# Gathering token rows by quarters and turning them on VectorE in front of six experts

## The chip, the cores and the metric

The kernel runs on one core of a Trainium2 chip. The metric is the device time of one execution in microseconds (us). The core has TensorE (PE, with its weight loads shown as PEld), VectorE (DVE), ScalarE (ACT), GpSimd (POOL) and SyncE (SP), which here issues most of the DMA transfers; GpSimd issues the transfers that go by a list of indices. A matmul reads its operands from SBUF and writes into one of eight banks of PSUM.

## The reference

An attention of the RWKV kind gives 4 x 768 = 3072 token rows of 8 x 48 = 384 channels. A router then picks one of eight experts for each token, and the expert is a two-layer network, applied with the router's weight:

```python
xn = x / (np.linalg.norm(x, axis=-1, keepdims=True) + 1e-06)
logits = xn @ en.T / tau                  # en: normalised expert embeddings, 8 x 384
expert_idx = np.argmax(logits, axis=1)
gate_w = softmax(logits)[np.arange(N), expert_idx]
for e in range(E):                        # 8 experts, F = 1024
    mask = expert_idx == e
    h = np.maximum(x[mask] @ w1[e], 0.0)  # w1[e]: 384 x 1024
    out[mask] = gate_w[mask, None] * (h @ w2[e])  # w2[e]: 1024 x 384
```

## The kernel before

The attention comes first, in 12 turns. Each finished chunk of token rows goes to a scratch array `xs` in DRAM (3072 x 384, f32) and through the router. When all tokens have an expert, VectorE has a list of token numbers for each expert, sorted by the experts' size: `take` holds, for expert e and tile t, the 128 token numbers of the tile, one per partition. `goes` holds where their results go.

The experts are worked off in this order with fixed capacities (CAPS, in tokens): 384, 384, 432, 416, 400, 384, 384, 384. Below, experts are numbered by it from 0 to 7. Experts 0 and 1 (`EARLY`) start before the last lists are there, and their first layer is done by plain products (L1065, L1070). Experts 2 to 7 take these steps:

- **Gather** (`gather`, L1037). GpSimd issues an indirect DMA per tile: up to 128 rows of 384 channels (1536 bytes) from `xs` into a tile G, token on partition. There are eight such tiles, four for even experts and four for odd ones.
- **Turn** (`turn_m`, L1134). A product contracts over partitions, so the channels have to come onto partitions: TensorE multiplies each 128 x 128 block of G by the identity, three column blocks m, into the PSUM banks Y. ScalarE copies each m to SBUF (`copy_x`, L1127) as `xTe[:, m, :]`.
- **First layer** (`group`, L1157). Two groups of 2 x 2 block products by Strassen's scheme, which needs sums of blocks of the weights (S, `sum_w1`) and of x (Tx, `sum_x`), both by VectorE in the helper at L1087. The results, after an add by VectorE and a relu by ScalarE, are hT (or RT, the same role for odd experts).
- **Second layer** (`layer2`). First the last tile's third (L1320) or, at over 384 tokens, its columns (L1327), then again Strassen's block products (L1290), with sums of h (RT on VectorE, `sum_h`) and of w2 (T, `sum_w2`). The adds at L1312 and a scaling at L1374 write y rows, which GpSimd scatters to the output (`send`, L1259).

The weights of an expert come by SyncE: w1 as three DMAs of 128 partitions x 1024 (512 KB each), w2 as four (L1023). Two sets of weight tiles alternate. Weights of expert e + 2 are issued when expert e's second layer has been written out.

The order of instructions on every engine is fixed by hand: `plan.at(t, f, ...)` files a step under a time, and `plan.emit()` writes the steps in order of these times. Each engine works its instructions off strictly in that order and waits for what an instruction needs. So a step's planned time says only where it stands in its engine's queue. In `experts` the turning of the next expert's x stands at the end of each expert's first layer (at + 0.0, 0.4, 2.7), around the third or the columns of the second layer. The matmuls that open a new accumulation take the next of six PSUM banks in a ring (`ring_bank`); the two banks Y are kept for the transposes.

Of the kernel before, what the change touches and what calls it, by code (L numbers as in the profile page):

```python
# [11 lines left out]
I32 = mybir.dt.int32  # L12
# [170 lines left out]
def build_consts(k):  # L183

    nc, pool = k.nc, k.const
    k.half = pool.tile([128, B], F32, name="half")
    nc.gpsimd.memset(k.half, 0.5)
    k.casts = []
    k.token = pool.tile([128, NCH, B], I32, name="token")
    nc.gpsimd.iota(k.token, pattern=[[C * B, NCH], [C, B]], base=0, channel_multiplier=1)  # L190

    k.ng = pool.tile([128, NCH, B, 2], F32, name="ng")
    k.rev = numbers(k, "rev", [128, E], [[-1, E]], E, 0)
    k.slot = numbers(k, "slot", [128, 128], [[1, 128]], 0, 0)
# [12 lines left out]
    k.rev_sorted = pool.tile([128, E], F32, name="rev_sorted")

    k.cum_oh = pool.tile([128, E, B + 1], F32, name="cum_oh")
    nc.gpsimd.memset(k.cum_oh[:, :, 0:1], 0.0)  # L210
    k.cum = k.cum_oh[:, :, 0]
    k.oh = k.cum_oh[:, :, 1:].rearrange("q x b -> q b x")
    k.on = pool.tile([128, E, B + 1], F32, name="on")
    nc.gpsimd.memset(k.on, 1.0)
    nc.gpsimd.memset(k.on[:, :, 0:1], 0.0)
    k.back = pool.tile([128, NCH, B], F32, name="back")
    k.rank = pool.tile([128, NCH, B], F32, name="rank")
    k.lists = pool.tile([128, E, 2, TM], F32, name="lists")
    nc.gpsimd.memset(k.lists[:, :, 0, :], float(SKIP))
    nc.gpsimd.memset(k.lists[:, :, 1, :], 0.0)  # L220
    k.lists_sorted = pool.tile([128, E, 2, TM], F32, name="lists_sorted")
    k.take = pool.tile([128, E, TM], I32, name="take")
    k.goes = pool.tile([128, E, TM], I32, name="goes")
    k.take_first = pool.tile([128, EARLY, AHEAD], I32, name="take_first")


def cast_consts(k):
# [525 lines left out]
        k.nc.vector.reduce_sum(k.take_first[:, :, i], t, axis=AX.X)  # L753


def goes(k):
    out_rows(k, k.goes, k.take, k.rt)

# [78 lines left out]
def attention(k):  # L837
# [115 lines left out]
    for t, fn, *args in (  # L953
        (14.1, logits, k, c),
        (15.2, take_logits, k, c),
        (16.1, turn_logits, k, c),
        (16.2, keep_logits, k, c),
        (16.6, choose, k, c, True),
        (18.0, ranks, k, c),
        (18.7, placed, k, c),  # L960
        (18.8, places, k, c),
        (18.6, choose_a, k, c),
        (19.0, scale, k, c),
        (19.9, rows_of, k, c),
        (20.25, exps, k, c),
        (20.9, gate, k, c),
        (21.0, values, k, c),
        (21.5, sort_lists, k),
        (l + 4.5, put, k, c),
        (l + 5.5, collect, k, c),  # L970
        (l + 5.6, goes, k),
        (l + 5.9, flags, k),
    ):
        plan.at(end + t, fn, *args)
# [24 lines left out]
    plan.at(P + 6.9, embeddings_a, k)  # L999
    plan.at(P + 8.7, cast_consts, k)  # L1000
    plan.at(2 * P + 6.0, embeddings_b, k)
    plan.at(2 * P + 6.6, embeddings_c, k)
    plan.at(2 * P + 7.6, decays, k)
    for i, G in enumerate(k.G):
# [8 lines left out]
def weights(k, j, which, pieces=None, paced=False):  # L1013

    w = k.weights[j][which]
    e = bass.ds(k.expert[j], 1)
    if which == 0:
        src, step = k.w1[e].rearrange("o (c p) f -> p (o c) f", p=128), 1
    else:
        src, step = k.w2[e].rearrange("o (f p) m -> p (o f) m", p=128), 2  # L1020
    all_pieces = range(0, src.shape[1], step)
    for m in all_pieces if pieces is None else all_pieces[pieces]:
        ins = k.nc.sync.dma_start(out=w[:, m : m + step], in_=src[:, m : m + step])  # L1023
        if paced:
            after(k, ins, k.last)
# [6 lines left out]
def gather(k, e, t):  # L1032
    n = rows_in(e, t)
    G = k.G[(e % 2) * TM + t]
    first = e < EARLY and t < AHEAD
    rows = (SETTLE[t] + 1) * B * C if first else N
    k.nc.gpsimd.indirect_dma_start(  # L1037
        out=G[0:n, :], out_offset=None, in_=k.xs[0:rows, :],
        in_offset=IndirectOffsetOnAxis(ap=(k.take_first if first else k.take)[0:n, e, t : t + 1], axis=0),
        bounds_check=rows - 1, oob_is_err=False,  # L1040
    )


# [73 lines left out]
def sum_x(k, e, i):  # L1117
# [3 lines left out]
        return  # L1121
    t = [k.T1[:, j, 0:h] for j in range(4)]
    right_sums(k, t, [[half_of(k, e, m, c) for c in range(2)] for m in range(2)], i)


def copy_x(k, e, m):
    k.nc.scalar.copy(x_of(k, e, m)[:, 0 : CAPS[e]], k.xbank[m][:, 0 : CAPS[e]])  # L1127


def turn_m(k, e, m):  # L1130
    ps = k.xbank[m] = k.Y[m % 2]
    for t in range(TILES[e]):
        G, r = k.G[(e % 2) * TM + t], rows_in(e, t)
        k.nc.tensor.transpose(  # L1134
            ps[:, t * 128 : t * 128 + r], G[0:r, m * 128 : (m + 1) * 128], k.ident[0:r, 0:r]
        )


def group(k, plan, e, g, at):
# [251 lines left out]

def experts(k):
    nc = k.nc
    k.turn = 5
    k.sent = 0
    k.outs = dram_disjoint_views(k.out, 4)
    k.xT = [k.gp1.tile([128, NK, max(CAPS)], F32, name=f"xTe{i}") for i in range(2)]
    wide = [k.gp1.tile([128, NF // 2, max(CAPS)], F32, name=f"hT{i}") for i in range(2)]
    rt = [x.rearrange("q u p s j i -> q (u p s j i)") for x in k.RT]
    k.h = [wide, [x.rearrange("q (f i) -> q f i", f=4) for x in rt[0:2]]]  # L1400
# [4 lines left out]
    k.T1 = k.gp1.tile([128, 5, max(CAPS) // 2], F32, name="Tx")  # L1405
    k.T2 = k.gp1.tile([128, 4, 4, 192], F32, name="T2")
    k.kept = [k.gp1.tile([128, max(CAPS)], F32, name=f"kept{i}") for i in range(3)]
    k.xbank = {}
    for e in range(EARLY):
        for t in range(AHEAD, TILES[e]):  # L1410
            turn_tile(k, e, t)
    for e in range(EARLY):
        for t in range(TILES[EARLY + e]):
            gather(k, EARLY + e, t)
    nc.gpsimd.drain()
    for e in range(EARLY):
        layer1_rest(k, e)
    plan = Plan()
    at = 0.0
    for e in range(E):  # L1420
        if e >= EARLY:
            for g in range(2):
                group(k, plan, e, g, at + g * GROUP * CAPS[e] / 384)
# [6 lines left out]
        nxt = {0: 2, 1: None}.get(e, e + 1)  # L1430
        if nxt is not None and nxt < E:
            for m in range(NK):
                plan.at(at + (0.0, 0.4, 2.7)[m], turn_m, k, nxt, m)
                plan.at(at + (0.45, 0.9, 3.0)[m], copy_x, k, nxt, m)
            for t in range(TILES[nxt + 1] if EARLY <= e and nxt + 1 < E else 0):
                plan.at(at + 3.1, gather, k, nxt + 1, t)
            for i in range(5):
                plan.at(at + (4.0, 5.8, 6.2, 7.6, 8.4)[i], sum_x, k, nxt, i)
            at += 0.9
# [273 lines left out]
def kernel(  # L1713
# [37 lines left out]
    sets = [weight_tiles(n, i) for i in range(2)]  # L1751
    n.weights = [sets[e % 2] for e in range(E)]
    n.expert = {}
    n.G = [n.const.tile([128, DM], F32, name=f"G{i}") for i in range(2 * TM)]

    with tc.manual_schedule(), ExitStack() as long_ctx:
        n.long = long_ctx.enter_context(tc.tile_pool(name="long", bufs=1))
# [39 lines left out]
```

## Time and profile before

| | us |
|---|---|
| median of 3 runs | 408.48 |
| lowest and highest | 408.22, 412.2 |
| the profiled execution | 407.85 |
| its span, first to last instruction | 406.0 |
| TensorE busy | 385.4 (95%) |
| VectorE busy | 227.0 (56%) |
| ScalarE busy | 146.0 (36%) |
| GpSimd busy | 130.6 (32%) |
| granted TensorE clock | 0.992 of full speed |

The profile's page shows one execution. Its groups of instructions name the source line, the engine, the operation, output <- inputs by the program's names, then count, busy time and what ended the idle time before them. "PE py L1134" in the chain of waits is work of TensorE into a tile named py by line 1134. A piece of the chain is given by its start, its length, what it is, and how many instructions it holds. In a timeline row, the number in brackets is the time for which the engine was idle before the instruction, and behind the arrow stands what it waited for. "issue" is time in which it waited for nothing that the profile shows. The line numbers in these rows are those of the kernel before; in the changed kernel the same code stands some 60 lines lower.

### The profile page before, as it was taken

How to read it: one execution, taken by the hardware profiler on the slowest of the kernel's cores; microseconds unless marked ns; L12 is line 12 of the kernel's file. 1: busy time of each engine (PE TensorE's matmuls, PEld its weight loads, DVE VectorE, ACT ScalarE, POOL GpSimd, SP SyncE). 2: the span in 40 equal slices, each digit the busy share in tenths (PEclk: the TensorE clock that was granted, in tenths of full speed). 3: DMA queues.
4: the chain of work that ended last, by engine and by line, in shares of the span. 5: the costliest groups of instructions: out<-in, count | busy, mean ns of one | idle time of the engine just before them, and what ended most of it. 6: DMA issues, size and time to landing. Idle time of an engine off the chain costs nothing.

```text
span 406.0 us, 12451 instructions
## 1 busy us (share of the span) xinstructions
PE 385.4 (95%) x5116; PEld 346.1 (85%) x5116; DVE 227.0 (56%) x578; ACT 146.0 (36%) x375; POOL 130.6 (32%) x167
## 2 busy tenths in 40 slices
PE   8879989899997999999999999999999999999993
PEld 4767879797887999978899999999998889979983
DVE  6866777788788380433752644546454464374331
ACT  3355554555462634321134214313413413413410
POOL 2765746474542231612151023104303412012001
PEclk9999999999998999999999999999999999999998
DMA  9998787777606357825743252424605553001001
GB/s 126 172 167 168 160 175 165 164 167 162 162 26 214 118 182 238 271 95 180 280 137 111 84 194 89 150 58 160 207 21 183 151 177 119 0 19 39 2 19 48
DMA packets 95460, 54.40 MB, mean 134 GB/s; under 512 B 78723, under 2 KB 90034, under 8 KB 95394
## 3 DMA queue, kind: packets, MB, share of 16 engines
q1 hardware_dynamic: 89634, 43.68, 42.1%
q0 software_dynamic: 3264, 9.44, 7.0%
q10 hardware_dynamic: 2496, 0.40, 0.8%
q8 instruction: 42, 0.69, 0.7%
q14 instruction: 24, 0.20, 0.1%
HBM read 44.20 MB, written 9.58 MB: 132 GB/s over the span
## 4 chain that ended last, share of the span: by engine, by line
PE 82%; DMA 4%; issue 3%; DVE 1%; POOL 0%; POOLq 0%; SPq 0%
PE ps L1157 15%; PE ps L1290 12%; PE pu L1157 8%; PE ps L1070 5%; PE pu L1290 5%; PE ps L371 4%; PE ps L1320 4%; PE ps L411 4%; PE ps L1327 3%; PE pu L536 3%; PE pu L1320 3%; PE py L502 2%; PE py L1070 2%; PE py L1134 2%; PE pu L447 2%
## 5 line engine op out<-in xcount | busy, mean ns | idle before, releaser
L1259 POOL DMA_INDIRECT out_dram<-y,goes x27 | 30.8, 1141 | 173.7 <-ACT y L1374 91.9
L1037 POOL DMA_INDIRECT G<-xs,take x23 | 24.4, 1061 | 29.4 <-PE py L1057 8.5
L1157 PE MATMUL ps<-xTe,w 128*128 128x192 f32 (+3 forms) x160 | 31.4, 333 | 0.0
L355 POOL TENSOR_TENSOR Rw<-R,rpow 128x384 f32<-128x384 f32 x22 | 23.1, 1051 | 16.6 <-PE ps L411 8.4
L1157 PEld LDWEIGHTS ps<-xTe,w 128*128 128x128 f32 x160 | 27.5, 190 | 0.0
L1312 DVE SCALAR_TENSOR_TENSOR y<-ps,lists_sorted,kept 128x192 f32<-128x192 f32 x18 | 7.1, 416 | 36.0 <-ACT kept L1304 22.2
L1070 PE MATMUL ps<-RT,w 128*128 128x128 f32 x204 | 26.2, 278 | 0.7 <-DVE RT L1060 0.4
L1290 PE MATMUL ps<-T,RT 128*128 128x192 f32 x144 | 26.0, 328 | 0.0
L1070 PEld LDWEIGHTS ps<-RT,w 128*128 128x128 f32 x204 | 24.2, 192 | 1.5 <-issue 0.6
L411 PE MATMUL ps<-RT,KT 48*64 48x128 f32 x768 | 25.0, 274 | 0.3 <-issue 0.2
L1290 PEld LDWEIGHTS ps<-T,RT 128*128 128x128 f32 x144 | 23.6, 190 | 0.6 <-ACT kept L1304 0.6
L411 PEld LDWEIGHTS ps<-RT,KT 48*64 48x64 f32 x768 | 21.0, 133 | 3.7 <-issue 2.7
L351 POOL TENSOR_TENSOR Kw<-K,kpow 128x384 f32<-128x384 f32 x22 | 23.5, 1068 | 0.0
L1157 PE MATMUL ps<-Tx,S 128*128 128x192 f32 (+3 forms) x96 | 20.3, 341 | 0.0
L387 ACT COPY RT<-ps 128x512 f32<-128x512 f32 x22 | 12.9, 586 | 19.9 <-PE ps L371 17.9
L1175 ACT COPY kept<-ps 128x384 f32<-128x384 f32 (+3 forms) x24 | 11.7, 490 | 22.7 <-PE ps L1157 19.7
L1087 DVE TENSOR_TENSOR RT<-ps,kept 128x384 f32<-128x384 f32 (+1 forms) x15 | 8.5, 566 | 19.9 <-PE ps L1157 19.9
L426 DVE TENSOR_TENSOR AT<-ps,smask 128x256 f32<-128x256 f32 x48 | 18.5, 413 | 1.1 <-PE ps L411 1.1
L398 DVE TENSOR_TENSOR RT<-ps,uw 128x512 f32<-128x512 f32 x22 | 15.2, 689 | 6.8 <-ACT RT L387 6.7
L371 PE MATMUL ps<-ident,Rw 128*128 128x128 f32 x96 | 15.4, 282 | 3.6 <-POOL Rw L355 1.6
L1127 ACT COPY xTe<-py 128x384 f32<-128x384 f32 (+3 forms) x18 | 8.8, 490 | 27.0 <-PE py L1134 26.9
L433 DVE COPY_PREDICATED AT<-dmask,ps 128x256 f32<-128x256 int32 x48 | 18.5, 439 | 0.0
(344 smaller groups left out, 889.9 us busy)
## 6 DMA issues: line engine op xcount, KB each, us to landing
w<-in_moe_w_dram SPq DMA_DIRECT2D x24, 512.0 KB, 4.5
w<-in_moe_w_dram SPq DMA_DIRECT2D x32, 384.0 KB, 3.6
xs<-X SPq DMA_DIRECT2D x24, 192.0 KB, 3.5
K<-in_k_dram SPq DMA_DIRECT2D x32, 96.0 KB, 3.6
R<-in_r_dram SPq DMA_DIRECT2D x32, 96.0 KB, 3.2
V<-in_v_dram SPq DMA_DIRECT2D x32, 96.0 KB, 3.6
V<-in_v_dram SPq DMA_DIRECT2D x8, 192.0 KB, 5.4
K<-in_k_dram SPq DMA_DIRECT2D x6, 192.0 KB, 5.4
```

Of the source, the lines that this page charges most:

```text
L351: q.tensor_mul(of(k.Kw, t)[:, u, :, 0:D], of(k.K, t)[:, u] if t else raw(k, 0)[:, u, :, 0:D], k.kpow)
L355: ins = k.nc.gpsimd.tensor_mul(of(k.Rw, t)[:, u, :, 0:D], of(k.R, t)[:, u], k.rpow)
L371: k.last = k.nc.tensor.transpose(bank[:, p * C : (p + 1) * C], pair(src[:, u], p), k.ident)
L411: ins = k.nc.tensor.matmul(k.D[2 * u + par][halves(s), p * C : (p + 1) * C], KT[rows, u, p, halves(s)], RT[rows, u, p, s].rearrange("q j i ...
L426: k.nc.vector.tensor_mul(of(k.AT, t)[:, u, par].rearrange("q (p i) -> q p i", p=NP), kinds(k, u, par)[:, :, 0], k.smask[:, None, :].to_bro ...
L433: k.nc.vector.copy_predicated(of(k.AT, t)[:, u, par].rearrange("q (p i) -> q p i", p=NP), k.dmask[:, None, :].to_broadcast([128, NP, HC]), ...
L1037: k.nc.gpsimd.indirect_dma_start(out=G[0:n, :], out_offset=None, in_=k.xs[0:rows, :], in_offset=IndirectOffsetOnAxis(ap=(k.take_first if f ...
L1070: k.last = k.nc.tensor.matmul(ps, w1[:, m, f * 128 : (f + 1) * 128], x_of(k, e, m)[:, cols], start=(m == 0), stop=(m == NK - 1))
L1157: k.last = nc.tensor.matmul(ps[:, i * h : (i + 1) * h], a[:, g, i * 128 : (i + 1) * 128], b, start=start and i == 0, stop=True, skip_group ...
L1259: k.nc.gpsimd.indirect_dma_start(out=out[:, :], out_offset=IndirectOffsetOnAxis(ap=k.goes[0:n, e, t : t + 1], axis=0), in_=y[0:n, :], in_o ...
L1290: k.last = nc.tensor.matmul(ps, a(q), b[:, q], start=start and q == 0, stop=True, skip_group_check=True,)
L1320: k.last = nc.tensor.matmul(p.z, h_one(k, e, f)[:, 256:384], w2[:, f, :], start=(f == 0), stop=(f == NF - 1))
```

## The change

For experts 2 to 7 the x rows are no longer turned by TensorE.

- Each row of `xs` is read as four quarters of 96 channels (384 bytes). One gather (`gather_group`) fetches 32 tokens: partition 32q + i receives quarter q of token i. An expert takes 12 to 14 such gathers (14, 13, 13, 12, 12, 12; 76 in all), where it took three or four of whole rows (21 in all).
- VectorE's transpose works within blocks of 32 x 32. After it (`fold_x`, three operations per expert, one per m) partition 32q + j holds channel 96q + 32m + j of each token: x with channels on partitions, though in another order than before.
- The first-layer weights of these experts are loaded in that same order: 12 DMAs of 32 partitions x 1024 (128 KB each) instead of three.
- The list of quarters is made once from `take`: a multiply on VectorE (`spread_a`), a matmul with a 0/1 matrix that repeats 32 tokens' numbers over the four partition groups (`spread_b`), and a step that forms 4 x token + q (`spread_c`). `build_fold` makes the constants by five VectorE operations during the attention.
- The gathers for expert e + 1 are filed in the first layer of expert e. Before, they were filed in the second layer of expert e - 1 (those of experts 2 and 3 ahead of everything). The eight G tiles are now two, one per parity, and an expert's gathers write into parts of one tile.
- The banks Y are free, and the ring holds all eight PSUM banks.

GpSimd's queue from the first gathers by `take` on. G_83 to G_90 are tiles of rows; the L1259 rows are the scatters of results. Before:

```order
L1037 DMA G_85<-xs,take 128x384
L1037 DMA G_89<-xs,take 128x384
L1037 DMA G_83<-xs,take 128x384
L1037 DMA G_84<-xs,take 128x384
...
L1259 DMA out_dram<-y,goes 3072x384 x6
L1037 DMA G_83<-xs,take 128x384
L1037 DMA G_84<-xs,take 128x384
L1037 DMA G_85<-xs,take 128x384
L1037 DMA G_86<-xs,take 16x384
L1259 DMA out_dram<-y,goes 3072x384 x2
```

And now, where L1089 is the gather of whole rows, L1099 that of quarters and L1317 the scatter:

```order
L1089 DMA G_83<-xs,take 128x384
L1089 DMA G_84<-xs,take 128x384
L1099 DMA G_83<-xs,quarters 128x96 x14
L1317 DMA out_dram<-y,goes 3072x384 x6
L1099 DMA G_84<-xs,quarters 128x96 x13
L1317 DMA out_dram<-y,goes 3072x384 x2
```

Eight gathers of experts 2 and 3 became 14 of expert 2 alone; the 13 of expert 3 stand behind the first six scatters.

VectorE's queue in the second layer of expert 0 (T are sums of w2 of expert 0, RT sums of its h, Tx sums of the x of expert 2). Before:

```order
L1087 TENSOR_TENSOR T_3230<-w_0_80,T_3230 128x768
L1087 TENSOR_TENSOR RT_115<-R_104,RT_115 128x256
L1087 TENSOR_TENSOR RT_115<-K_99,RT_115 128x256
L1087 TENSOR_TENSOR Tx<-xTe_3223 128x216
L1087 TENSOR_TENSOR T_3230<-w_0_80 128x768
```

And now, where L1109 is the fold and L1158 the helper of the sums:

```order
L1109 STREAM_TRANSPOSE xTe_3232<-G_83 128x448 x2
L1158 TENSOR_TENSOR T_3239<-w_0_80,T_3239 128x768
L1158 TENSOR_TENSOR RT_109<-R_98,RT_109 128x256
L1158 TENSOR_TENSOR RT_109<-K_93,RT_109 128x256
L1109 STREAM_TRANSPOSE xTe_3232<-G_83 128x448
L1158 TENSOR_TENSOR Tx<-xTe_3232 128x216
L1158 TENSOR_TENSOR T_3239<-w_0_80 128x768
```

Two folds stand ahead of the second T sum and a third ahead of the first Tx.

TensorE's queue at the same place, the end of expert 1's first layer and the start of expert 0's second. Before:

```order
L1070 MATMUL ps_59<-RT_114,w_1_81 128x128 x3
L1134 MATMUL py_64<-ident,G_83 128x128
...
L1134 MATMUL py_65<-ident,G_86 128x48
L1320 MATMUL ps_58<-w_0_80,R_102 128x384 x2
...
L1134 MATMUL py_64<-ident,G_86 128x48
L1290 MATMUL ps_59<-w_0_80,R_102 128x192 x2
```

And now:

```order
L1141 MATMUL ps_59<-RT_108,w_1_81 128x128 x3
L1378 MATMUL ps_58<-w_0_80,R_96 128x384 x2
...
L1378 MATMUL ps_58<-w_0_80,K_93 128x384 x2
L1348 MATMUL ps_59<-w_0_80,R_96 128x192 x2
```

The twelve transposes are gone, and the products follow one another.

The diff:

```diff
+QUARTER = DM // 4
+GROUPS = [-(-n // TS) for n in CAPS]
+WIDE = max(GROUPS) * TS
...
+def build_fold(k):
+    nc, pool = k.nc, k.const
+    k.fold = pool.tile([128, 4, TS], F32, name="fold")
+    one = k.aconst.tile([128, TS], F32, name="of_32")
+    nc.vector.reduce_sum(one, k.ident.rearrange("q (g i) -> q i g", g=4), axis=AX.X)
+    nc.vector.tensor_copy(k.fold, one[:, None, :].to_broadcast([128, 4, TS]))
...
+def spread_a(k):
+    shape = [128, E - EARLY, TM, 4]
+    k.by_four = k.rt.tile(shape, F32, name="by_four", tag="by_four", bufs=1)
+    k.nc.vector.tensor_mul(
+        k.by_four, k.take[:, EARLY:, :, None].to_broadcast(shape), k.of_4[:, None, None, :].to_broadcast(shape)
+    )
+def spread_b(k):
+    ps = k.U[0][:, 0 : (E - EARLY) * TM * 4]
+    k.nc.tensor.matmul(
+        ps, k.fold.rearrange("q g i -> q (g i)"), k.by_four.rearrange("q x t g -> q (x t g)"), start=True, stop=True
+    )
+def spread_c(k):
+    flat = "q x t g -> q (x t g)"
+    ps = k.U[0][:, 0 : (E - EARLY) * TM * 4]
+    k.nc.vector.tensor_scalar(k.quarters.rearrange(flat), ps, 4.0, k.fourth, ALU.mult, ALU.add)
...
     (l + 5.5, collect, k, c),
+    (l + 5.55, spread_a, k),
     (l + 5.6, goes, k),
+    (l + 6.5, spread_b, k),
+    (l + 6.6, spread_c, k),
     (l + 5.9, flags, k),
...
+    plan.at(3 * P + 8.9, build_fold, k)
...
 def weights(k, j, which, pieces=None, paced=False):
+    if which == 0 and j >= EARLY:
+        src = k.w1[e].rearrange("o (q c i) f -> c (o q) i f", q=4, c=NK)
+        for m in range(NK):
+            for q in range(4):
+                k.nc.sync.dma_start(out=w[q * TS : (q + 1) * TS, m], in_=src[m, q])
+        return
...
+def gather_group(k, e, g):
+    t, i = divmod(g, 4)
+    k.nc.gpsimd.indirect_dma_start(
+        out=k.GG[e % 2][:, g * QUARTER : (g + 1) * QUARTER], out_offset=None,
+        in_=k.xs.rearrange("n (q c) -> (n q) c", q=4),
+        in_offset=IndirectOffsetOnAxis(ap=k.quarters[:, e - EARLY, t, i : i + 1], axis=0),
+        bounds_check=4 * N - 1, oob_is_err=False,
+    )
+def fold_x(k, e, m):
+    n = GROUPS[e]
+    k.nc.vector.transpose(
+        k.xT[e % 2][:, m, 0 : n * TS].rearrange("q (g i) -> q g i", i=TS),
+        k.GG[e % 2][:, 0 : n * QUARTER].rearrange("q (g m i) -> q m g i", g=n, m=NK)[:, m],
+    )
...
 def ring_bank(k):
-    k.turn = (k.turn + 1) % 6
-    return (*k.D, *k.U)[k.turn]
+    k.turn = (k.turn + 1) % 8
+    return k.bank[k.turn]
...
-    for e in range(EARLY):
-        for t in range(TILES[EARLY + e]):
-            gather(k, EARLY + e, t)
+    for g in range(GROUPS[EARLY]):
+        gather_group(k, EARLY, g)
...
+        if EARLY - 1 <= e < E - 1:
+            for g in range(GROUPS[e + 1] if e >= EARLY else 0):
+                plan.at(at + 1.0 + 0.01 * g, gather_group, k, e + 1, g)
...
-                plan.at(at + (0.0, 0.4, 2.7)[m], turn_m, k, nxt, m)
-                plan.at(at + (0.45, 0.9, 3.0)[m], copy_x, k, nxt, m)
-            for t in range(TILES[nxt + 1] if EARLY <= e and nxt + 1 < E else 0):
-                plan.at(at + 3.1, gather, k, nxt + 1, t)
+                plan.at(at + (2.6, 3.0, 3.4)[m], fold_x, k, nxt, m)
```

More of the change, by code (lines that the diff above doesn't have):

```diff
@@ L224, in build_consts @@
     k.take_first = pool.tile([128, EARLY, AHEAD], I32, name="take_first")
+    k.quarters = pool.tile([128, E - EARLY, TM, 4], I32, name="quarters")
+def build_fold(k):
[4 more added lines that the diff above has]
+    nc.vector.tensor_copy(k.fold, one[:, None, :].to_broadcast([128, 4, TS]))
+    k.of_4 = pool.tile([128, 4], F32, name="of_4")
+    nc.vector.reduce_sum(k.of_4, k.ident.rearrange("q (g i) -> q g i", g=4), axis=AX.X)
+    k.fourth = pool.tile([128, 1], F32, name="fourth")
+    four = k.aconst.tile([128, 4], F32, name="four")
+    nc.vector.tensor_mul(four, k.of_4, k.slot[:, 0:4])
+    nc.vector.reduce_sum(k.fourth, four, axis=AX.X)
 def cast_consts(k):
@@ L1123, in sum_x @@
     right_sums(k, t, [[half_of(k, e, m, c) for c in range(2)] for m in range(2)], i)
[L1126 to L1136, printed above, removed]
 def group(k, plan, e, g, at):
@@ L1393, in experts @@
     nc = k.nc
-    k.turn = 5
+    k.turn = 7
     k.sent = 0
     k.outs = dram_disjoint_views(k.out, 4)
-    k.xT = [k.gp1.tile([128, NK, max(CAPS)], F32, name=f"xTe{i}") for i in range(2)]
+    k.xT = [k.gp1.tile([128, NK, WIDE], F32, name=f"xTe{i}") for i in range(2)]
     wide = [k.gp1.tile([128, NF // 2, max(CAPS)], F32, name=f"hT{i}") for i in range(2)]
@@ L1407, in experts @@
     k.kept = [k.gp1.tile([128, max(CAPS)], F32, name=f"kept{i}") for i in range(3)]
-    k.xbank = {}
     for e in range(EARLY):
@@ L1753 @@
     n.expert = {}
-    n.G = [n.const.tile([128, DM], F32, name=f"G{i}") for i in range(2 * TM)]
+    n.GG = [n.const.tile([128, TM * DM], F32, name=f"G{i}") for i in range(2)]
+    n.G = [G[:, t * DM : (t + 1) * DM] for G in n.GG for t in range(TM)]
     with tc.manual_schedule(), ExitStack() as long_ctx:
```

## The prediction

> **What bounds the kernel now.** I read the page first: its table of engines, then the by-engine shares of the chain that ended last.
> ```profile
> PE 385.4 (95%) x5116; PEld 346.1 (85%) x5116; DVE 227.0 (56%) x578; ACT 146.0 (36%) x375; POOL 130.6 (32%) x167
> PE 82%; DMA 4%; issue 3%; DVE 1%; POOL 0%; POOLq 0%; SPq 0%
> ```
> TensorE (PE) is busy for 385.4 of 406.0 us, and the chain lies on it for 82%. So work taken off TensorE shortens the kernel, as long as nothing it then needs comes later. Next I read the chain by line from 160 us to the end, and its pieces around the first expert's second layer (start, length, what).
> ```profile
> by line: PE ps L1157 25.4%; PE ps L1290 19.3%; PE pu L1157 12.8%; PE pu L1290 8.2%; PE ps L1320 6.4%; PE ps L1327 5.6%; PE pu L1320 4.2%; PE ps L1070 3.9%; issue 3.6%; PE py L1134 3.2%; PE pu L1327 2.6%; PE py L1070 1.2%; PE ps L1386 0.5%;
> 173.64 1.19 PE py L1134 x8
> 174.82 5.36 PE ps L1320 x16
> 180.18 0.52 PE py L1134 x4
> 180.69 4.42 PE ps L1290 x26
> ```
> The transposes of L1134 lie on the chain at two places before each of experts 2 to 7, back to back with products. 3.2% of 246 us is 7.9 us; that is what the change takes away.
>
> **Part 1, TensorE: 63 transposes go.** The gain is the full 7.9 us only if no wait was hidden behind them. The last expert has no successor to transpose for, so its chain shows the same step without them:
> ```profile
> 375.82 8.93 PE ps L1157 x52
> 384.75 5.16 PE pu L1320 x16
> ```
> 375.82 + 8.93 = 384.75: the second layer starts with no gap. So -7.9 us. The 18 ScalarE copies that go with them cost nothing: ScalarE is 36% busy.
>
> **Part 2, GpSimd (POOL): 76 gathers instead of 21.** Here are the gathers of before (start, length, idle time before), and the time from issue to landing.
> ```profile
> 150.02 1.12 POOL L1037 DMA_INDIRECT G<-xs,take  x1 [0.30 <-issue]
> 163.51 1.17 POOL L1037 DMA_INDIRECT G<-xs,take  x1 [0.30 <-issue]
> 167.92 1.00 POOL L1037 DMA_INDIRECT G<-xs,take  x1 [0.30 <-PE ps L1070]
> 169.22 0.91 POOL L1037 DMA_INDIRECT G<-xs,take  x1 [0.30 <-issue]
> DMA to landing us min/median/max: 3.0/3.5/7.2
> ```
> The pitch from 163.51 to 169.22, four gathers on, is 5.71 / 4 = 1.43; the shortest is 1.00 + 0.30 = 1.30. So 12 to 14 gathers last 16 to 20 us, where before three or four lasted 4 to 6. VectorE's first fold of an expert waits for the last of them, and each later operation on VectorE waits behind it. Call the pitch p. Two places are tightest.
>
> *The first expert (14 gathers).* They need the list of quarters.
> ```profile
> 152.53 0.13 DVE L1675 CAST flag<-far 1x1 int32<-1x1 f32 x1
> 161.97 0.56 DVE L1060 COPY RT<-py 128x384 f32<-128x384 f32 x1 [9.31 <-PE py L1057]
> 162.91 0.95 DVE L1087 TENSOR_TENSOR T<-w 128x768 f32<-128x768 f32 x1
> 166.99 0.43 DVE L1087 TENSOR_TENSOR RT<-K,RT 128x256 f32<-128x256 f32 x1
> 174.78 0.38 DVE L1087 TENSOR_TENSOR Tx<-xTe 128x216 f32<-128x216 f32 x1 [7.37 <-ACT xTe L1127]
> ```
> The list is VectorE's next work after 152.53; with two more small operations (about 0.2 each) and a handover it is there at about 153.35 (estimate). The 14th gather starts at 153.35 + 13p and lands 3.5 later. From landing VectorE has three folds (estimated from the COPY of 384 columns at 0.56: 0.55 each, 1.7 together), two T sums (0.95 each, pitch 0.87), two RT sums (0.43, pitch 0.34) and one Tx (0.38) to do: some 4.6 us. TensorE needs the T sum at 180.69 plus the first eight products (a third of the 4.42 over 26, 1.36), minus the transposes gone (1.19 + 0.52): 180.3. So the loss is 153.35 + 13p + 3.5 + 4.6 - 180.3 = 13p - 18.8. VectorE idles 9.31 us up to 161.97, so six gathers run at 1.30; seven at 1.43 make 13p = 17.8, and the fold is 1.0 us early. The landing may take longer, since DMA is fuller here (length, then TensorE, its loads, VectorE, ScalarE, GpSimd, clock, DMA share, GB/s):
> ```profile
> 162.00:172.00 10.00, 9.59 (x86) 9.38 (x85) 5.42 (x12) 3.61 (x13) 6.40 (x6) 1.00 0.87 276
> 172.00:182.00 10.00, 10.00 (x51) 7.17 (x50) 3.62 (x8) 2.39 (x6) 0.89 (x1) 1.00 0.29 109
> ```
> The last gather is issued at 171 and flies in the emptier stretch. Between 0 and 2.7 (landing 7.2), I take +0.3.
>
> *Experts 5 and 6 (12 gathers for the next expert).* These start behind the scatter of the expert before:
> ```profile
> 307.40 1.42 POOL L1259 DMA_INDIRECT out_dram<-y,goes  x1 [0.30 <-DVE y L1312]
> 339.36 1.44 POOL L1259 DMA_INDIRECT out_dram<-y,goes  x1 [0.30 <-DVE y L1312]
> 323.00 0.66 PE py L1134 x6
> 353.88 0.66 PE py L1134 x6
> 357.71 0.35 DVE L1087 TENSOR_TENSOR Tx<-xTe 128x192 f32<-128x192 f32 x1
> 360.85 0.68 DVE L1087 TENSOR_TENSOR S<-w 128x512 f32<-128x512 f32 x1
> 366.61 0.74 DVE L1312 SCALAR_TENSOR_TENSOR y<-ps,lists_sorted,kept 128x192 f32<-128x192 f32 x2 [3.15 <-ACT kept L1304]
> 368.04 1.46 PE L1290 MATMUL ps<-T,hT 128*128 128x192 f32 x8
> ```
> The product at 368.04 writes into a bank that the add at 366.61 reads. In the new kernel it is due 368.04 - 353.88 - 0.99 (six and three transposes) = 13.2 us after the first layer's end. From landing to the end of that add VectorE has three folds (1.7), an RT sum, five Tx at a pitch of 0.3 and a y of 0.6 (2.7), four S at 0.63 (2.5) and the add (0.4): 7.3. So the landing may be 5.9 us behind the first layer's end. For expert 6: 339.36 + 1.44 + 0.30 + 11p + 3.5 - (353.88 + 5.9) = 11p - 15.2. For expert 5 likewise 11p - 16.3. Beside these gathers VectorE makes four T sums of 0.95, and such neighbours slow a gather:
> ```profile
> 211.05 1.59 POOL L1037 DMA_INDIRECT G<-xs,take  x1 [0.30 <-issue]
> 211.67 0.95 DVE L1087 TENSOR_TENSOR T<-w,T 128x768 f32<-128x768 f32 x1
> ```
> 1.59 against 0.91 to 1.00 with VectorE idle, 0.6 more. Four times 0.5 over 12 gathers puts p at 1.31 + 0.17 = 1.48: expert 6 loses 1.1 us, expert 5 nothing. Experts 2 to 4, in whose second layers TensorE needs the same results later, I put at 0.
>
> The Trainium skill, SBUF — State Buffer, section Who interferes with whom, says that VectorE and GpSimd share one pair of ports as an exclusive lock, that a VectorE operation with two SBUF inputs contends with a GpSimd instruction that reads SBUF, and that one with at most one SBUF input (outside the two-port modes) does not. The row of 1.59 agrees with the first two. By that rule the folds, with one input, leave the gathers alone and the sum is as above; if the lock held for them too, the slower case below would gain ground.
>
> **Part 3, VectorE: 18 folds.** Six times 1.7 = 10 us more on an engine busy 56%, in stretches where it waited (7.37 us idle before 174.78). Nothing in the trace transposes on VectorE. Ends: 0.56 (the copy) and 1.1 (the same work twice); I take 0.56, since a fold reads and writes each element once as the copy does. At 1.1 each place loses 1.7 us more landing time.
>
> Once, in the attention, VectorE also builds the fold's matrix: five operations before the masks of a turn.
> ```profile
> 48.39 0.88 DVE L643 TENSOR_TENSOR l<-l,inv 128x32 f32<-128x32 f32 x1
> 49.86 0.77 DVE L433 COPY_PREDICATED AT<-dmask,ps 128x256 f32<-128x256 int32 x2
> 51.08 0.19 DVE L775 TENSOR_REDUCE rank<-full 128x4 f32<-128x32 f32 x1
> 50.74 1.02 PE ps L371 x8
> 52.95 1.27 issue
> ```
> By the small reduction (0.19, 32 inputs) five take about 1.1 with 128 inputs in some. TensorE's L371 at 50.74 needs the banks that L433 frees at 50.63, so up to 1.0 is lost; the 1.27 of issue at 52.95 may take it up again. Between 0 and 1.0 I take +0.35.
>
> **Part 4, the rest at 0.** The one product that spreads the list (128 by 96) fits into a wait of TensorE's for weights, 0.29 us:
> ```profile
> 151.07 0.49 PE L1070 MATMUL ps<-RT,w 128*128 128x128 f32 x2 [0.29 <-DMA w<-in_moe_w_dram]
> L1023 SPq DMA_DIRECT2D w<-in_moe_w_dram x12: 333/360/388, 167.9 to 196.7; - x12
> 197.30 0.69 DVE L1087 TENSOR_TENSOR S<-w 128x512 f32<-128x512 f32 x1
> ```
> Uncovered it would cost about that 0.3. SyncE issues 12 pieces of the first-layer weights instead of 3: at 0.36 plus some 0.15 around it, 9 more are 4.6 us per expert. The first such issue is at 167.9 and VectorE first sums these weights at 197.30, 29 us later; behind the pieces only later weights are queued. Two more banks in the ring can only free TensorE earlier. Scatters now stand behind 12 to 14 gathers on GpSimd, but none is read again before the end.
>
> **The sum** is -7.9 + 0.3 + 1.1 + 0.35 = -6.15. Against the profiled execution: 407.85 - 6.15 = 401.7. The median shown is 408.48, 0.63 higher; I predict 401.8.
>
> **The rivals.**
> *A, gathers or folds somewhat late.* p of 1.55 everywhere gives 1.4 + 0.75 + 1.85 = 4.0 instead of the 1.4 in the sum: 404.3. Folds of 1.1 each instead of 0.56 use up the first expert's 1.0 and 0.7 over, and cost 1.6 more at expert 5 and at 6: 401.7 + 3.9 = 405.6. For it speaks that the slack is 1 us in 18. Against it, the pitch of 1.30 with VectorE idle. Chance 0.19.
> *B, slower: GpSimd can't keep up.* If each gather took the 1.59 of its slowest row, p = 1.89, and the three places lose 5.8 + 4.5 + 5.6 = 15.9: 407.85 - 7.9 + 0.35 + 15.9 = 416, and more if experts 2 to 4 are late too. It decides from 35p - 50.3 = 7.55, that is p = 1.65. For it: the 1.59 row, many more VectorE operations beside gathers, descriptors of 384 bytes that no row of before shows. Against it: only one gather in four is slowed in the rows, and a T sum of 0.95 covers one at most. Chance 0.14.
> *C, a wait takes the transposes' place.* They cover 1.2 us between the last sums of the first layer and the second; if the new kernel waits there for ScalarE or VectorE, and only half of the 7.9 is kept, 4.0 more: 405.7. The last expert's rows speak against it. Chance 0.06.
> That the transposes stay on TensorE I exclude: the new order of its instructions has none of them.
>
> **How the numbers follow.** My case has 0.61 and its own range is 399.9 (nothing lost) to 403.8. A reaches from 403.5 to 407, C 404 to 407, B from 408 to 424. About 1% (4.1 us) is what a measurement of this kernel can tell from no change. Below 404.4: 0.61 and a quarter of A and C, 0.67. Within 1% (404.4 to 412.6): the rest of A and C and a little of B, 0.20. Slower: 0.13. The range that holds 8 in 10 runs from 399.8 to 407.5: B and a little of A and C lie above it.
>
> **What would show it.** No transposes between the first layer and L1378, whose first product follows without a gap (Part 1); gathers of 1.0 to 1.2 us with 0.30 between, and the last of the 14 issued near 171 (Part 2); folds of 0.5 to 0.65 (Part 3); TensorE waiting for a T sum near 180 by under 1 us, and near 367 by about 1 us. It is wrong if TensorE waits several us for VectorE behind a fold in each expert, or if gathers are longer than 1.35 on the mean.

## The result, and the profile after

| | before | after |
|---|---|---|
| median, us | 409.0 (408.22 to 412.2) | 396.77 (395.63 to 398.25) |
| profiled execution, us | 407.85 | 398.25 |
| its span, us | 406.0 | 396.4 |

The ratio is 0.9689, with a 95% interval of 0.9623 to 0.9755: the kernel became faster, by some 12 us where 6.7 were forecast. 396.77 lies below the forecast range of 399.8 to 407.5. Four later comparisons of the same two kernels gave ratios of 0.9719, 0.9621, 0.9732 and 0.9771, so the first one is near the middle of what the change does, if rather on the good side.

The new kernel's page shows the engines, and the groups of the gathers and of the folds:

```profile
PE 376.9 (95%) x5055; PEld 340.9 (86%) x5055; DVE 237.1 (60%) x603; ACT 138.4 (35%) x357; POOL 189.5 (48%) x222
L1099 POOL DMA_INDIRECT G<-xs,quarters x76 | 81.1, 1068 | 24.8 <-issue 21.3
L1109 DVE STREAM_TRANSPOSE xTe<-G 128x384 f32<-128x384 f32 (+2 forms) x18 | 10.0, 583 | 21.8 <-DMA G<-xs,quarters 18.0
```

TensorE is busy 8.5 us less, GpSimd 59 us more, and neither GpSimd nor VectorE became the bound. A fold takes 0.58 us. These are the pieces of its chain at the places that the prediction quoted (start, length, what):

```profile
171.74 1.34 PE ps L1141 x12
173.08 5.16 PE ps L1378 x16
178.24 9.36 PE ps L1348 x56
366.14 8.93 PE ps L1215 x52
375.08 5.16 PE pu L1378 x16
```

The products of the second layer follow those of the first with no gap. Between two places that both kernels have, the end of expert 1's first layer and the last expert's second layer, before took 384.75 - 173.64 = 211.11 us, and after 375.08 - 173.08 = 202.00: 9.1 us less. Ahead of that stretch the new kernel is 0.6 us earlier, and behind it both take the same 21.3 us. In this pair of profiles, then, almost all of the 9.6 us of span is gained in the experts. That is already more than the 7.9 that stood on the chain. And the medians differ by 12 us, not by 9.6.

The gathers of the first expert, and VectorE's T sum beside one of them, its first folds and the T sum behind them (start, length, idle time ahead):

```profile
152.36 0.99 POOL L1099 DMA_INDIRECT G<-xs,quarters  x1 [1.94 <-DVE quarters L795]
162.76 1.41 POOL L1099 DMA_INDIRECT G<-xs,quarters  x1 [0.30 <-issue]
169.72 1.00 POOL L1099 DMA_INDIRECT G<-xs,quarters  x1 [0.30 <-issue]
DMA to landing us min/median/max: 2.4/2.6/6.0
```

```profile
162.36 0.95 DVE L1158 TENSOR_TENSOR T<-w 128x768 f32<-128x768 f32 x1
173.72 1.17 DVE L1109 STREAM_TRANSPOSE xTe<-G 128x448 f32<-128x448 f32 x2 [8.40 <-DMA G<-xs,quarters]
177.14 0.95 DVE L1158 TENSOR_TENSOR T<-w 128x768 f32<-128x768 f32 x1
```

The first expert's pitch is (169.72 - 152.36) / 13 = 1.34. Over all 76 gathers the landing takes 2.6 us in the median instead of 3.5, but the first fold begins 4.0 us behind the start of this last gather. The T sum is ready at 178.09, where TensorE needs it at 178.24 + 1.30 = 179.5.

### The profile page after: what moved, and what is told of

It reads as the page before. It is cut to its first block, busy times and chain, and to the rows that moved or that the text cites. A ratio compares the mean times of both kernels' runs of the same rounds, so it can differ in the third digit from the quotient of the medians.

```text
span 396.4 us, 12661 instructions
## 1 busy us (share of the span) xinstructions
PE 376.9 (95%) x5055; PEld 340.9 (86%) x5055; DVE 237.1 (60%) x603; ACT 138.4 (35%) x357; POOL 189.5 (48%) x222
## 4 chain that ended last, share of the span: by engine, by line
PE 80%; DMA 3%; issue 3%; DVE 2%; POOL 1%; SPq 1%; ACT 0%; POOLq 0%; DVEq 0%
PE ps L1215 13%; PE ps L1348 8%; PE py L1215 6%; PE ps L1141 5%; PE pu L1215 5%; PE pu L1348 5%; PE ps L391 4%; PE ps L1378 4%; PE py L1348 3%; PE ps L431 3%; PE ps L1385 3%; PE pu L1378 3%; PE py L522 2%; PE py L1141 2%; PE pu L556 2%
## 5 line engine op out<-in xcount | busy, mean ns | idle before, releaser
L1099 POOL DMA_INDIRECT G<-xs,quarters x76 | 81.1, 1068 | 24.8 <-issue 21.3
L1317 POOL DMA_INDIRECT out_dram<-y,goes x27 | 30.6, 1133 | 104.4 <-ACT y L1432 47.2
L375 POOL TENSOR_TENSOR Rw<-R,rpow 128x384 f32<-128x384 f32 x22 | 22.8, 1036 | 14.5 <-PE ps L431 8.2
L1215 PE MATMUL ps<-xTe,w 128*128 128x192 f32 (+3 forms) x132 | 25.9, 334 | 0.0
L1141 PEld LDWEIGHTS ps<-RT,w 128*128 128x128 f32 x204 | 24.7, 195 | 1.3 <-issue 0.6
L371 POOL TENSOR_TENSOR Kw<-K,kpow 128x384 f32<-128x384 f32 x22 | 23.7, 1079 | 0.5 <-DMA R<-in_r_dram 0.5
L1109 DVE STREAM_TRANSPOSE xTe<-G 128x384 f32<-128x384 f32 (+2 forms) x18 | 10.0, 583 | 21.8 <-DMA G<-xs,quarters 18.0
L1215 PEld LDWEIGHTS ps<-xTe,w 128*128 128x128 f32 x132 | 22.7, 190 | 0.0
L494 POOL TENSOR_TENSOR T<-T,wC 128x384 f32<-128x384 f32 x10 | 8.3, 827 | 27.8 <-DVE T L488 27.8
L391 PE MATMUL ps<-ident,Rw 128*128 128x128 f32 x96 | 15.8, 289 | 4.6 <-DVE AT L453 2.9
L1348 PE MATMUL ps<-T,RT 128*128 128x192 f32 x96 | 17.5, 329 | 0.0
L1362 ACT ACTIVATE kept<-ps,lists_sorted 128x192 f32<-128x192 f32 x12 | 5.1, 421 | 35.2 <-PE ps L1348 35.2
L1348 PEld LDWEIGHTS ps<-T,RT 128*128 128x128 f32 x96 | 15.7, 190 | 0.6 <-ACT kept L1362 0.6
L1215 PE MATMUL ps<-Tx,S 128*128 128x192 f32 (+3 forms) x76 | 16.1, 343 | 0.0
L391 PE MATMUL ps<-ident,Kw 128*128 128x128 f32 x96 | 15.1, 280 | 0.9 <-issue 0.5
```

Of the source, the lines that this page charges most:

```text
L371: q.tensor_mul(of(k.Kw, t)[:, u, :, 0:D], of(k.K, t)[:, u] if t else raw(k, 0)[:, u, :, 0:D], k.kpow)
L375: ins = k.nc.gpsimd.tensor_mul(of(k.Rw, t)[:, u, :, 0:D], of(k.R, t)[:, u], k.rpow)
L391: k.last = k.nc.tensor.transpose(bank[:, p * C : (p + 1) * C], pair(src[:, u], p), k.ident)
L1099: k.nc.gpsimd.indirect_dma_start(out=k.GG[e % 2][:, g * QUARTER : (g + 1) * QUARTER], out_offset=None, in_=k.xs.rearrange("n (q c) -> (n q ...
L1141: k.last = k.nc.tensor.matmul(ps, w1[:, m, f * 128 : (f + 1) * 128], x_of(k, e, m)[:, cols], start=(m == 0), stop=(m == NK - 1))
L1215: k.last = nc.tensor.matmul(ps[:, i * h : (i + 1) * h], a[:, g, i * 128 : (i + 1) * 128], b, start=start and i == 0, stop=True, skip_group ...
```

## The experiments

**1. The two kernels once more.** No edit.

> The kernel before, once more, for a second profile of it. In the two profiles at hand the new kernel reaches its first router product (L536 before, L556 after) at 33.3 us and the kernel before at 35.6 us, 2.3 us apart, ahead of any line that the change touches on the critical path. Theory 'chance': the start of the attention differs from run to run of the same kernel; here L536 first comes anywhere between 33 and 36. Theory 'layout or code': the kernel before always comes at 35.6 +- 0.3.

> The new kernel, once more. Theory 'chance' for the start: L556 first comes between 33 and 36 us, and the time from there to the first scatter is what counts. Theory 'layout or code': 33.3 +- 0.3 again. From the end of expert 1's first layer to the last expert's first third (173.08 to 375.08 us in the first profile, 202.0) I expect 202.0 +- 0.3 in either case. Ratio to the kernel before 0.965 to 0.975.

The kernel before came to the end of its setup at 34.16 us again (34.19 in the first profile); the new one at 33.42 (31.88 in the first). So neither theory fits: the kernel before is regular, and the new one is earlier both times, but its first router product, expected at 33.3 +- 0.3, came at 34.83. The windows show one difference. For the kernel before, the first two stretches of 10 us (after the length: PE, PEld, DVE, ACT, POOL busy, clock, DMA share, GB/s):

```profile
0.00:10.00 10.00, 8.31 (x50) 5.05 (x54) 7.09 (x18) 3.89 (x9) 2.70 (x14) 1.00 1.02 125
10.00:20.00 10.00, 8.38 (x257) 6.59 (x251) 8.71 (x22) 3.60 (x9) 7.36 (x11) 1.00 1.28 172
```

And for the new kernel:

```profile
0.00:10.00 10.00, 8.24 (x30) 4.81 (x30) 6.59 (x17) 3.12 (x7) 3.08 (x15) 1.00 0.94 157
10.00:20.00 10.00, 9.68 (x279) 8.10 (x280) 9.61 (x25) 4.54 (x14) 8.44 (x12) 1.00 1.08 191
```

The same transfers, issued in the same order, move 157 GB/s instead of 125. The new kernel's ratio was 0.9719 (0.967 to 0.9768); its experts took 376.94 - 174.66 = 202.28 us, those of the kernel before 387.45 - 176.34 = 211.11.

**2. The transposes alone.** The kernel before, without the transposes and their copies: experts 2 to 7 work on another x.

```diff
-                plan.at(at + (0.0, 0.4, 2.7)[m], turn_m, k, nxt, m)
-                plan.at(at + (0.45, 0.9, 3.0)[m], copy_x, k, nxt, m)
...
+    for x in k.xT:
+        nc.gpsimd.tensor_copy(x[:, :, 0:384], k.early_x[0][:, :, 0:384])
+        nc.gpsimd.tensor_copy(x[:, :, 384:432], k.early_x[1][:, :, 0:48])
```

> The kernel before without the 63 transposes of experts 2 to 7 and their 18 copies: xT is filled once from the early experts' x, so the x of experts 2 to 7 is not theirs. All gathers of whole rows stay. It gives the price of the transposes alone. Theory 'pieces': the chain's pieces of L1134 are the price, 7.9 us, so about 0.981. Theory 'pieces and handover': each of the 12 stretches of transposes also lengthens the product behind it by some 0.1 to 0.2 (5.36 and 1.50 with, 5.16 and 1.30 without), so 9.1 us from 173.64 to 384.75 and about 0.978. If the ratio is 0.97 or below, the removal has a further effect on its own.

The ratio was 0.9783 (0.9733 to 0.9833). Its chain:

```profile
174.67 5.16 PE ps L1320 x16
376.67 5.16 PE pu L1320 x16
```

376.67 - 174.67 = 202.00: the transposes cost 9.1 us, and no wait appeared in their place. The new kernel, with its gathers and folds, takes the same 202.00. The 1.2 us beyond their own pieces are in the products behind them. In the kernel before, where expert 4's x (400 rows, the last tile with 16) is turned:

```profile
256.81 1.13 PE py L1134 x8
257.93 2.37 PE pu L1327 x16
260.30 0.49 PE py L1134 x4
260.79 1.50 PE pu L1290 x8
```

The same two stretches of products in the new kernel:

```profile
252.10 2.17 PE pu L1385 x16
254.27 1.30 PE pu L1348 x8
```

Each stretch of products behind a turn is 0.20 longer. Where all tiles are full (expert 5: 291.31, 1.96 us, against 283.94, 1.96 us) it is not. Experts 2, 3 and 4 have a short last tile and two such stretches each: 6 x 0.2 = 1.2, and 7.95 + 1.2 = 9.1.

**3. Four more gathers per expert.** They fetch the same rows into a spare tile; each stands ahead of one of the expert's own gathers.

```diff
 def gather_group(k, e, g):
     t, i = divmod(g, 4)
+    if g < 4:
+        extra(k, e, g)      # the same gather into spare_rows
```

> The new kernel with four more gathers per expert (of the same rows into a spare tile), ahead of its own: 100 instead of 76, 1.3 us each, so the last gather of an expert is issued 5.2 us later. Theory 'the folds have 1.4 to 1.8 us to spare' (first expert: T sum ends 178.09, product due 179.54; last: adds could end 358.36 and end 357.36, of which 0.77 is a wait for ScalarE): each of the six experts loses 3.4 to 3.8 us, in all 18 to 23 us. Rival 'much slack, only the transposes counted': under 6 us. Rival 'GpSimd is the bound already': 31 us, all of 6 x 5.2.

It took 425.64 us, in a single run. The experts took 401.91 - 175.22 = 226.7 us, 24.7 more than 202.0, or 4.1 for each of the six; 18 to 23 were expected. In the second layers of experts 2 to 6 TensorE waits once or twice, mostly for an add that stands behind the folds on VectorE (in brackets the wait):

```profile
243.16 2.89 PE L1363 MATMUL ps<-T,hT 128*128 128x192 f32 x8 [2.05 <-DVE y L1385]
348.53 2.46 PE L1363 MATMUL ps<-T,RT 128*128 128x192 f32 x8 [3.68 <-DVE y L1385]
383.65 2.93 PE L1363 MATMUL pu<-T,hT 128*128 128x192 f32 x8 [3.27 <-DVE y L1385]
```

Not all of the 24.7 us is waiting. TensorE was busy for 210.1 of the 226.7 us, against 201.8 of 202.0 in the new kernel: 16.6 us are waits, and 8.3 are products that took longer, at a granted clock of 0.97 on the mean instead of 1.00. Behind the first wait shown, eight products took 2.89 us, where eight of the same kind at 312.57 took 1.57. This is that window (after the length: PE, PEld, DVE, ACT, POOL busy, clock, DMA share, GB/s):

```profile
243.16:246.05 2.89, 2.89 (x9) 2.89 (x10) 1.64 (x4) 0.00 (x0) 0.00 (x0) 0.51 0.45 169
```

In the order of the experts (0, then 2 to 6) the waits were 3.0, 2.1, 1.0, 2.5, 4.6 and 3.3 us. The first expert's last gather was 5.2 us later than in the new kernel, as expected, so the gathers had some 0.6 us to spare at expert 5, about 2 at the first expert and at expert 6, and 2.7 to 4.2 elsewhere. The mechanism of the slower rival is there. With four gathers more, the new kernel is slower than the old, which took 409.66 us beside it.

**4. The place of the attention's tiles.** An unused constant shifts everything behind it. Its size was the only edit: 240 words in the kernel before, 16 or 56 in the new one.

```diff
+    pool.tile([128, 240], F32, name="pad")
     k.take = pool.tile([128, E, TM], I32, name="take")
```

With the new constants, the change had moved the attention's tiles K, R, V, Kw and Rw, with all that lies behind the constants, by 960 bytes or more within a partition. V, Kw and Rw hold 192-byte pieces, one in every 256 bytes; they stood 96 bytes behind a multiple of 256, and now stand 32 behind.

> The kernel before with an unused constant of 960 bytes per partition, so that the attention's tiles (K, R, V, Kw, Rw) stand where they stand in the new kernel: the 192-byte pieces written into V, Kw and Rw then start 32 bytes behind a multiple of 256 instead of 96, and no longer cross one. Theory 'place': from 0 to 10 us the DMA moves 156 GB/s instead of 125 with the same engines' share or less, L536 first comes at 32 to 34.5 us, and the kernel is 1 to 3 us faster (0.993 to 0.998). Rival 'not the place' (something else in the new kernel, or the transfers' order): 125 GB/s, 1.000 within its interval.

> The kernel before without the transposes and copies of experts 2 to 7 (their x is not theirs), and with the 960 bytes. If the transposes and the place of the attention's tiles are the whole of the change's gain, this is as fast as the new kernel: 0.969 to 0.972. If the new kernel has a further source, this stays at 0.974 to 0.978.

> The new kernel with an unused constant of 64 bytes per partition: V, Kw and Rw start 96 bytes behind a multiple of 256 again, as in the kernel before, and cross the next one. Theory 'place': 125 GB/s from 0 to 10 us, L556 first at 35.5 to 36, and 1 to 3 us slower than the new kernel (0.974 to 0.978 of the kernel before, like the one without transposes). Rival 'not the place': 156 GB/s, 0.969 to 0.972.

> The new kernel with an unused constant of 224 bytes per partition: V, Kw and Rw start at a multiple of 256, K and R at one of 64, so that two of four pieces of K and R cross a 256-byte line instead of three. Theory 'place, and crossing is what costs': at least 156 GB/s from 0 to 10 us, perhaps 170 to 180, and 0 to 2 us faster than the new kernel. If only a start at 32 or 96 differ by something else: like one of the two.

The kernel before with 960 bytes:

```profile
0.00:10.00 10.00, 8.21 (x66) 5.25 (x66) 7.81 (x20) 4.43 (x11) 3.22 (x15) 1.00 0.88 154
10.00:20.00 10.00, 8.89 (x280) 7.58 (x280) 9.24 (x23) 3.92 (x11) 9.14 (x13) 1.00 0.99 187
31.54 0.06 DVE tau L264
```

It has the new kernel's rate and comes to the end of its setup at 31.54 instead of 34.2; its ratio was 0.9909 (0.9874 to 0.9944). The new kernel with 64 bytes fell back to 125 GB/s and to 34.41 us. So the place of the tiles sets the rate, and the theory "place" stands. At a multiple of 256 (224 bytes) the rate was 160, hardly better than at 32 behind (152 to 157). Without transposes and with the 960 bytes, the kernel before had 0.9672 (0.96 to 0.9744): as fast, against the kernel before, as the new kernel elsewhere. The Trainium skill, DMA: Bandwidth & Descriptors, section How a descriptor splits into AXI transactions, says that a transaction can read less than 256 bytes but must start at a 256-byte-aligned address. 192 bytes from 96 on cross such a line and from 32 or 0 on do not; the rates of 125 against 154 and 160 agree. But the page speaks of reads, and these pieces are written to the addresses in question: that they are split there is not shown.

But the two shifted new kernels took 422.36 and 419.22 us, ratios of 1.0265 (1.0181 to 1.035) and 1.0161 (1.0088 to 1.0234), which neither theory had: their experts needed 218.2 and 221.6 us. ScalarE issued late there, while gathers ran, and TensorE waited for it. ("issue" and "remote" both mean that the profile names nothing it waited for.) With 64 bytes, ScalarE:

```profile
220.81 0.52 ACT L1234 COPY kept<-ps 128x432 f32<-128x432 f32 x1 [1.36 <-issue]
221.22 0.57 ACT L1243 ACTIVATE hT<-hT 128x432 f32<-128x432 f32 x1
224.82 0.52 ACT L1234 COPY kept<-ps 128x432 f32<-128x432 f32 x1 [3.03 <-remote]
```

and TensorE:

```profile
222.21 0.89 PE L1216 MATMUL pu<-Tx,S 128*128 128x216 f32 x4
225.39 1.00 PE L1216 MATMUL ps<-xTe,S 128*128 128x216 f32 x4 [2.29 <-issue]
```

**5. Is that loss due to the place of the lists?** Two edits, each by itself: the tile of quarters allocated behind the fold's constants, or the unused constant (16 or 56 words) put there.

```diff
-    k.quarters = pool.tile([128, E - EARLY, TM, 4], I32, name="quarters")
...
     nc.vector.reduce_sum(k.fourth, four, axis=AX.X)
+    k.quarters = pool.tile([128, E - EARLY, TM, 4], I32, name="quarters")
```

```diff
     nc.vector.reduce_sum(k.fourth, four, axis=AX.X)
+    pool.tile([128, 16], F32, name="pad")
```

> The new kernel with the list of quarters 1248 bytes further on and the fold's constants in its place; every other tile stands where it stood. In the two kernels with an unused constant ahead of the lists, ScalarE issued late only while gathers by quarters ran (for nothing that the profile shows), and TensorE lost some 16 us. Theory 'the list's place': the same losses here, above 410 us. Theory 'the place of what lies behind (weights, attention tiles)': no losses, 395 to 399 us, 202 us from the end of expert 1's first layer to the last third.

> The new kernel with the unused 64 bytes behind the lists and the fold's constants, so that only weights and the attention's tiles shift. Theory 'the list's place': no late issue on ScalarE, 202 us in the experts, but the slow start of the attention (125 GB/s from 0 to 10 us), so 397 to 402 us. Theory 'the place of what lies behind': 16 us lost as with the 64 bytes ahead, above 412 us.

> The new kernel with 224 unused bytes behind the lists: attention pieces at a multiple of 256. Theory 'the list's place': no late issue, the fast start (160 and 190 GB/s), and within 1 us of the new kernel. Theory 'the place of what lies behind': above 412 us.

> The new kernel a third time, on the chip of this call, as the reference for the three others: 0.965 to 0.975 of the kernel before, 202 us from the end of expert 1's first layer to the last third, and 154 to 157 GB/s from 0 to 10 us. If chips differ, and not the places, this one too loses 16 us in the experts.

They took 399.2, 403.31, 400.74 (ratio 0.9745, 0.9692 to 0.9798) and 397.87 us (0.9621, 0.9539 to 0.9703), with no late ScalarE in any. So neither place makes the loss on this chip. On the rate, these runs narrow the place: with the unused bytes behind the lists it was 126 GB/s (64 bytes) and 159 (224 bytes), so what counts lies behind the lists and the fold's constants. For the loss, two things were left: the place of lists and constants together, or the other chip.

> The new kernel again, beside the two that lost 16 us in the experts. Theory 'the place of the lists and constants together': 395 to 400 us, no late issue on ScalarE. Theory 'that chip or call': if this call's chip is like that one, some 16 us more, as for the two others.

> The new kernel with 64 unused bytes ahead of the lists, again. Theory 'the place of the lists and constants together': 418 to 424 us again, ScalarE issuing late for some 13 us while gathers by quarters run. Theory 'that chip or call': 397 to 403 us, like the 64 bytes behind the lists.

> The new kernel with 224 unused bytes ahead of the lists, again. Theory 'the place of the lists and constants together': 415 to 424 us again. Theory 'that chip or call': 395 to 401 us.

401.47 us (0.9732, 0.9665 to 0.9799), 402.41 us (0.9748, 0.9679 to 0.9818) and 400.86 us: the same two programs lost nothing this time. The place alone does not make the loss, then. It came on that one chip, and only in the two kernels that gather by quarters; the two with whole rows, beside them, lost nothing. The new kernel itself did not run there, so whether it would lose there, or only with a shifted place, is open.

**6. How much each is worth.** Five rounds of three kernels on one chip.

> The kernel before with the 960 bytes again, in five rounds beside the next two, to size what the place of the attention's tiles is worth. By the first comparison 0.991 (0.987 to 0.994), 3.8 us; by the start alone (34.2 against 31.5 us) 2.6 us, 0.994; by the new kernel with and without 64 bytes ahead, 0.9 us, 0.998.

> The kernel before without transposes and copies (the x of experts 2 to 7 is not theirs), with the 960 bytes. 9.1 us below the kernel with the 960 bytes alone: 0.968 to 0.975. If transposes and place are all that the new kernel gains, the new kernel comes out within 1 us of this one, or later by what late folds and the fold's constants cost (0 to 1.2 us).

> The new kernel beside the two. Equal to the one without transposes and with the 960 bytes, or up to 1.2 us later, if these two are all of its gain; more than 1 us earlier if it has a further source.

| kernel | median, us | ratio | experts, us |
|---|---|---|---|
| before | 411.27 | 1 | not profiled here |
| with the 960 bytes | 409.59 | 0.9926 (0.9889 to 0.9963) | 386.56 - 175.44 = 211.1 |
| and without transposes | 400.44 | 0.9724 (0.9674 to 0.9774) | 376.06 - 174.07 = 202.0 |
| new | 402.46 | 0.9771 (0.9728 to 0.9815) | 380.00 - 177.69 = 202.3 |

The place is worth 1.7 to 3.0 us here (3.8 in experiment 4) and the transposes 9.1. The new kernel is 2.0 us behind the third. In the two profiles, which are 3.1 us apart, it comes to the experts 177.69 - 174.07 = 3.6 us later and loses 0.3 in them. So the loss lies in the attention. The chain of the new kernel (first profile) shows a place:

```profile
46.20 0.88 DVE l L663
47.08 0.31 DVE of L237
47.42 0.67 DVE fold L238
48.08 0.21 DVE of L240
48.31 0.67 DVE four L243
49.01 0.16 DVE fourth L244
49.16 0.66 DVE AT L446 x2
50.32 1.94 PE ps L391 x8
```

The fold's constants (L237 to L244) are on the chain with 2.0 us. From the end of the setup (the row of tau) to the router product behind (L556, in the others L537) the new kernel took 23.4, 23.5, 22.3, 23.5 and 23.6 us in its five profiles, the kernels with the 960 bytes 22.8, 22.5, 21.8 and 21.8: on the mean 1.0 us more.

Most of that is not the wait itself. The kernel before waited for 1.0 to 1.3 us behind these products (the 1.27 of issue at 52.95 that the prediction quoted), and the new one no longer does, so that wait is taken up. But the eight products of L391 took 1.94 us where the prediction's row of L371 has 1.02. TensorE had waited 2.05 us for the masks, and the granted clock fell to half behind it (the products, then the window):

```profile
50.32 1.09 PE L391 MATMUL ps<-ident,Rw 128*128 128x128 f32 x4 [2.05 <-DVE AT L453]
50.00:52.00 2.00, 1.68 (x8) 1.57 (x8) 1.97 (x8) 0.55 (x1) 0.00 (x0) 0.50 0.58 108
```

In the third profile of the new kernel, with a wait of 1.52 us, the clock stayed at 1.00:

```profile
51.31 0.63 PE L391 MATMUL ps<-ident,Rw 128*128 128x128 f32 x4 [1.52 <-DVE AT L453]
51.31 1.06 PE ps L391 x8
```

That is the profile with 22.3, level with the kernels with the 960 bytes. In the other four the clock fell to 0.50 somewhere between 50 and 54 us.

## Why the prediction was wrong

The direction was right and the size was not: 6.7 us were forecast and some 12 came. Three terms erred the same way: the place of tiles, which had none (1.7 to 3.8 us), the late folds (1.1 to 1.4) and the transposes (1.2). Only the constants erred the other way (0.65). Step by step:

- **Part 1, -7.9 for the transposes: 9.1.** The mechanism was right: they left the chain, no gap took their place (so rival C fell), and the last expert's rows were the right evidence. The term was mis-sized. It was the sum of the pieces named L1134, and left out the 0.2 us by which six stretches of products behind them were longer. One of them could be read from the rows quoted: 5.36 for sixteen products against 5.16 in the last expert.
- **Part 2, +1.4 for late folds: 0 to 0.6.** In the first profile TensorE waits for no fold, neither near 180 nor in expert 6. The pitch was 1.34 at the first expert and 1.31 in expert 6, where 17.8 / 13 = 1.37 and 1.48 were taken: one to three gathers of an expert took over 1.1 us, not four. In expert 6 the first fold began 2.8 us behind the start of the last gather, where 3.5 were taken from rows four times as long; at the first expert it was 4.0, so there the landing was no help. Put into the prediction's own limits, the measured pitches (1.40 in expert 5) leave 1.4, 0.9 and 0.8 us to spare at the first expert, at 5 and at 6; experiment 3 shows some 2.2, 0.6 and 1.9, and there these three places had the longest waits. So the limits hold roughly. Expert 4, put at 0, is tight too when landings are long: in the third profile of the new kernel, where two took 4.8 us or more, TensorE lost 0.3 us there to such an add. Rival B had a mechanism that exists, but gathers took 1.07 us on the mean, not 1.59.
- **Part 2's rule from the Trainium skill on the shared port.** The gather at 162.76 with 1.41 us runs beside the T sum at 162.36, and those with VectorE idle take 0.99 to 1.00: the trace agrees. The size varies more than the 0.5 us taken: the gather at 270.20 took 1.04 beside the T sum at 270.70, the one at 274.17 took 2.23 beside that at 274.58. The folds start after the last gather, so they show nothing on it.
- **Part 3, folds of 0.56: right** (0.58). **The constants, +0.35: about 1.0.** Five operations took 2.0 us, not 1.1. The later wait took up TensorE's, as Part 3 thought it might; what it did not have is the granted clock of 0.50 behind the wait (experiment 6).
- **Part 4, the rest at 0: the step that failed.** The change also moved the attention's tiles in memory, which no term of the sum had. By experiments 4 and 6 that is worth 1.7 to 3.8 us, the largest error of all.

Put together by the experiments: -9.1 for the transposes, -1.7 to -3.8 for the place, +1.0 for the constants, +0.3 for folds (the middle of 0 to 0.6), in all -9.5 to -11.6 us or 0.972 to 0.977 of 409 us. The five measured ratios are 0.9621 to 0.9771, on the mean 0.971. The sum falls short of the two best, 0.9689 and 0.9621, by up to 4 us, and what those had beyond it is not shown. The profiles cannot split the attention finer: between 100 and 140 us the granted clock was 0.87 to 1.00 from one profile to the next, both in kernels with transposes and in kernels without.

## What to carry to other kernels

Where an instruction goes from the critical path, compare the work behind it with the same work elsewhere: its price is not only its own row. A change that adds or resizes constants moves every tile behind them; before the rest is costed, look at how the pieces that DMA writes lie to lines of 256 bytes. A chain of gathers in front of an operation that a whole queue waits behind has a limit that can be worked out; here, in the tightest expert, it lay less than one gather (1.3 us) away. And a wait of TensorE's can cost more than its own length: look at the granted clock behind it (experiments 3 and 6).

## What the runs showed of the hardware

- The same transfers of 192-byte pieces ran at 124 to 126 GB/s in the first 10 us with V, Kw and Rw at 96 bytes behind a multiple of 256, in six profiles of four kernels, and at 152 to 160 with 32 or 0 behind.
- A gather takes GpSimd 1.00 us in the median and 0.30 to the next, whether its rows have 1536 bytes or 384, and up to 2.23 beside VectorE's sums; the smaller ones land in 2.6 instead of 3.5 us in the median.
- The two stretches of products behind transposes with a short last tile (48, 32 or 16 rows) were 0.2 us longer each, those behind full tiles were not. Why was not tried.
- Behind waits of 1.5 to 3.7 us TensorE often ran for some 2 to 5 us at a granted clock of 0.50 to 0.62, but not always: behind one of 1.52 (third profile) and one of 2.49 (experiment 3) it did not.
- On one chip, two kernels with gathers by quarters needed 16 to 20 us more in the experts, with ScalarE issuing late, and the same programs did not on another. The cause stays open.
